# A column of 1e-9 behind the rows of scores, in fixed tiles, in a windowed attention with two MLPs

## The chip, the core and the metric

The kernel runs on one core of a Trainium2 chip. The metric is the device time of one execution in microseconds (us); the time of a version is the median of its runs. The core has five engines with instruction streams of their own: PE (TensorE, matrix products; its weight loads are listed as PEld), DVE (VectorE), ACT (ScalarE), POOL (GpSimd) and SP (SyncE, which here only issues DMAs). Each engine works through its stream in order, and an instruction that waits for another engine or for a DMA holds up all that stands behind it on its own engine.

## The reference

```python
scores = scale * np.matmul(q, k.transpose(0, 1, 3, 2))        # q, k, v: 4 x 8 heads x 576 x 64
mask_plain = (rel >= 0) & (rel < 32)                          # heads 0 to 3
mask_dil = (rel >= 0) & (rel < 128) & (rel % 4 == 0)          # heads 4 to 7
scores = np.where(masks, scores, -1e9)
scores = scores - np.max(scores, axis=-1, keepdims=True)
attn = np.exp(scores)
attn = attn / (np.sum(attn, axis=-1, keepdims=True) + 1e-09)  # the 1e-9 of this change
x = np.matmul(attn, v)                                        # as 2304 tokens x 512
h = x @ w_in;  x = np.maximum(0.01 * h, h) @ w_out            # 512 -> 2048 -> 512
a = x @ w1;  b = x @ w2;  out = ((a * b) @ w3) @ w_out2       # 512 -> 1024 -> 1024 -> 512
```

q and k are scaled up so that the scores spread widely. Inputs are float64 in memory, the output is float32.

## The kernel before

**Stages.** The attention is cut into 32 groups of rows, n = 0 to 31: two heads by one half of the 576 positions, which is 5 or 4 blocks of 64 queries, each against 96 keys (KB = 96). A group's scores are a tile s of 128 partitions by 5 (or 4) blocks by 96. The first MLP runs between the groups: hidden products (ps_h), Prelu on ACT into g, the split of g into two parts of reduced precision (gs: a CAST and a subtraction, line 116 and 118), and the product with w_out (ps_x). Behind the last groups, between the remaining parts of the first MLP, the second MLP's last two weights begin to be multiplied together (w3 by w_out2, products ps_wp).

**One group.** `score_steps` multiplies q by k (ps_s, L420), scales and masks into s (DVE, L435), takes the negated maximum nmax (DVE, L440), and then goes one of two ways. The 14 groups listed in ONE_EXP subtract the maximum on POOL (L443), take the exponential of the whole tile in one ACT instruction (L448), and sum the rows on DVE (L453). The other 18 take one ACT instruction for each block, with the maximum as bias, and ACT sums the row along the way (L456, accum_out). `normalize_steps` adds 1e-9 to the sums (DVE, L464), takes the reciprocal (DVE, L467) and multiplies s by it (POOL, L469). `turn_p` turns s with PE (ps_p, L485) and copies it to pT (L489), and `value_steps` multiplies by v (ps_o, L506) and writes x (L529, L532).

**Memory.** Tiles come from pools of SBUF, stacked from the left and from the right. `edge` is the outermost pool on the right and stays; before, it holds one unused tile of 96 bytes a partition. Inside it lies `att`: masks first (1,728 bytes a partition), then qT and kT (two each, 2,304 bytes), three slots for s (1,920 bytes each) and the small nmax, total and rec, then pT, v and nat. Slots of a tag are handed out in turn. Where the string START has the sign `^`, `att` is closed, and the pool `fold` is opened over the same bytes. Its first tiles are rawf (two slots of 4,096 bytes, raw words of w3), wo2f (two of 2,048 bytes, rows of w_out2), and wo2 (the split w_out2). A transfer or a write into such a tile waits for whatever last used the bytes under it.

**Order.** All of this up to the second MLP is issued by hand: every letter of the string START is one step of a stage, and every L takes the next letter of LOADS, which names a load for SP. So no scheduler moves anything; the order on each engine is that of the code. After `^` come seven loads: rawf0 and rawf1 (four DMAs each, L670) and then five of wo2f (L680). Of the steps behind, `p` is the CAST of wo2f into wo2 on ACT (L116) and `r` its remainder on DVE (L118); `0`, `1`, `2`, ... turn rawf into rf and w3T (POOL L113, ACT L165 and L167, DVE L154, L171 and L702, then ACT L116 and DVE L118); `W` is the product ps_wp; `H`, `g`, `c`, `l` are the hidden product, Prelu and split of the first MLP, and `J` its second product.

Of the kernel before, what the change touches and what calls it, by code (L numbers as in the profile page):

```python
# [8 lines left out]
F32 = mybir.dt.float32  # L9
# [8 lines left out]
ALU = mybir.AluOpType  # L18
AX = mybir.AxisListType
# [5 lines left out]
EPS = 1.0e-9  # L25
# [3 lines left out]
def tile_window_attention_two_mlps(  # L29
# [14 lines left out]
    nc = tc.nc  # L44
    P = 128
# [21 lines left out]
    QB, KB = 64, 96  # L67
    NQ = HS[0] // QB
# [5 lines left out]
    def pool(name, side):  # L74
        es = ExitStack()
        return es, es.enter_context(
            tc.tile_pool(name=name, bufs=1, side=side, reuse_waits="tile")
        )

    const = ctx.enter_context(tc.tile_pool(name="const", bufs=1, side="left"))  # L80
    edge = ctx.enter_context(tc.tile_pool(name="edge", bufs=1, side="right"))
    edge.tile([P, 24], F32, name="edge")
    psum_es = ExitStack()
    psum = psum_es.enter_context(tc.tile_pool(name="psum", bufs=1, space=PSUM, reuse_waits="tile"))
    win_es, win_p = pool("win", "left")
# [12 lines left out]
    def side_bank(name):  # L98
        return psum.tile([P, 512], F32, tag="side", name=name, bufs=2)
# [82 lines left out]
    ONE_EXP = (0, 1, 3, 6, 11, 13, 16, 17, 19, 20, 27, 28, 29, 31)  # L182
# [108 lines left out]
    def pair(pi):  # L291
        b, h0 = divmod(pi, HP)
        return b, 2 * h0, 2 * h0 < H // 2
# [60 lines left out]
    def first_key(i, plain):  # L354
        k0 = max(i * QB - WINDOW, 0)
        g0 = i * QB // SR * SR
        return k0 if plain else max(k0, g0)
# [47 lines left out]
        qk_t[nm, pi] = dst  # L405
        yield

    sm = {}

    def score_steps(n):  # L410
        pi, r = order[n]
        plain = pair(pi)[2]
        qt, kt = qk_t["q", pi], qk_t["k", pi]
        bl = R_BLOCKS[r]
        nb = len(bl)
        ps = side_bank(f"ps_s{n}")[:, : nb * KB].rearrange("p (i k) -> p i k", k=KB)
        for i in bl:
            for j in range(2):
                d = slice(j * D, (j + 1) * D)
                nc.tensor.matmul(  # L420
                    ps[j * QB : (j + 1) * QB, i - bl.start],
                    qt[d, i * QB : (i + 1) * QB],
                    kt[d, first_key(i, plain) : first_key(i, plain) + KB],
                    start=True, stop=True,
                )
        yield
        s = att.tile([P, NQ, KB], F32, tag="s", name=f"s{n}", bufs=3)[:, :nb]
        if plain:
            cut = 1 if r == 0 else 0
            spans = [(0, cut, masks[:, :cut])] if cut else []  # L430
            spans.append((cut, nb, masks[:, 1:2].to_broadcast([P, nb - cut, KB])))
        else:
            spans = [(0, nb, masks[:, bl.start : bl.stop])]
        for a, z, mk in spans:
            nc.vector.scalar_tensor_tensor(  # L435
                s[:, a:z], ps[:, a:z], SCALE, mk, op0=ALU.mult, op1=ALU.add
            )
        yield
        nmax = att.tile([P, NQ], F32, tag="nmax", name=f"nmax{n}", bufs=2)
        nc.vector.tensor_reduce(nmax[:, :nb], s, op=ALU.max, axis=AX.X, negate=True)  # L440
        yield
        if n in ONE_EXP:
            nc.gpsimd.tensor_tensor(  # L443
                s, s, nmax[:, :nb].unsqueeze(2).to_broadcast([P, nb, KB]), op=ALU.add
            )
        yield
        if n in ONE_EXP:
            nc.scalar.activation(s, s, AF.Exp)  # L448
            yield
        total = att.tile([P, NQ], F32, tag="total", name=f"total{n}", bufs=2)  # L450
        sm[n] = (s, total[:, :nb])
        if n in ONE_EXP:
            nc.vector.tensor_reduce(total[:, :nb], s, op=ALU.add, axis=AX.X)  # L453
            yield
        for i in range(nb):
            nc.scalar.activation(  # L456
                s[:, i], s[:, i], AF.Exp, bias=nmax[:, i : i + 1], accum_out=total[:, i : i + 1]
            )
        yield
        yield  # L460

    def normalize_steps(n):
        s, total = sm[n]
        nc.vector.tensor_scalar(total, total, EPS, None, op0=ALU.add)  # L464
        rec = att.tile([P, NQ], F32, tag="rec", name=f"rec{n}", bufs=2)
        nb = s.shape[1]
        nc.vector.reciprocal(rec[:, :nb], total)  # L467
        yield
        nc.gpsimd.tensor_tensor(  # L469
            s, s, rec[:, :nb].unsqueeze(2).to_broadcast([P, nb, KB]), op=ALU.mult  # L470
        )
        yield
# [833 lines left out]
    with ExitStack():  # L1306
        make_identity(nc, ident)
        att_es, att = pool("att", "right")
        mask_d = masks = att.tile([P, S // QB, KB], BF16, name="masks")
        nc.vector.memset(masks, 0.0)  # L1310
        def build_masks():


            def band(m, shift):
                for j in range(2):
                    mj = m[j * QB : (j + 1) * QB]
                    for base, sign in ((shift, 1), (WINDOW - 1 - shift, -1)):
                        nc.gpsimd.affine_select(
                            out=mj, in_=mj, compare_op=ALU.is_ge, fill=NEG, base=base,
                            pattern=[[-sign, KB]], channel_multiplier=sign,  # L1320
                        )

            shifts = [i * QB - first_key(i, False) for i in range(S // QB)]
            band(mask_d[:, 0], shifts[0])
            band(mask_d[:, 1], WINDOW)
            m = mask_d[:, 2:]
            nc.vector.tensor_copy(m, mask_d[:, 1:2].to_broadcast(list(m.shape)))
            for i in range(2, S // QB):
                if shifts[i] != WINDOW:
                    nc.vector.memset(mask_d[:, i], 0.0)  # L1330
                    band(mask_d[:, i], shifts[i])

                x = ((i * QB) // SR + 1) * SR - first_key(i, False)
                if x < KB:
                    for j in range(2):
                        mj = mask_d[j * QB : (j + 1) * QB, i, :x]
                        nc.gpsimd.affine_select(
                            out=mj, in_=mj, compare_op=ALU.is_ge, fill=NEG, base=x - shifts[i] - 1,
                            pattern=[[0, x]], channel_multiplier=-1,
                        )  # L1340
# [90 lines left out]
        def late_turn(i):  # L1431
# [4 lines left out]
            "TY": turn_rows,  # L1436
            "F": late_turn,
            "SMXqEw": score_steps,
            "RN": normalize_steps,
            "PC": turn_p,  # L1440
            "Vxy": value_steps,
# [17 lines left out]
        with tc.manual_schedule():  # L1459
            warm = bank2("warm")  # L1460
            build_masks()
            feed, QK = iter(LOADS), "0123456789ABCDEFGHIJKLMNOPQRSTUV"
            wo2_no = iter(range(NI * NI // NG))
            begun = {}
            for x in START:
# [38 lines left out]
                else:  # L1504
# [3 lines left out]
                    if at == 0:  # L1508
                        n = len(done[-1])
# [52 lines left out]
```

## Time and profile before

| | |
|---|---|
| median of 3 runs | 815.05 us (815.03 to 818.45) |
| the profiled execution | 814.0 us, span 812.2 us |
| mean granted TensorE clock | 0.999 |
| PE busy | 798.0 us, 98% of the span |
| DVE busy | 535.8 us, 66% |
| ACT busy | 418.2 us, 51% |
| POOL busy | 195.9 us, 24% |

The span runs from the first to the last instruction of the profiled execution; its own time is 1.8 us longer. All rows below are of this one execution. A row of a timeline gives the start in us, the duration in us (of all instructions, where it ends in x and a count), the engine, the line, the operation, the tile written and the tile read, and in square brackets the idle time of the engine just before and what ended it. SPq are the DMA issues on SP.

### The profile page before, as it was taken

The page shows a single profiled execution, that of the slowest core. Times are in us where ns is not written, and L with a number is a line of the kernel's source. Part 1 is how long each engine was busy: PE and PEld are TensorE (multiplying, and loading weights), DVE is VectorE, ACT ScalarE, POOL GpSimd, SP SyncE. Part 2 cuts the span into 40 slices and gives each one's busy share as a digit, 9 for nine tenths or more (in the row PEclk, how much of TensorE's full clock was granted, in tenths as well). Part 3 has the DMA queues.
Part 4 walks back from the last instruction along what each step waited for, and adds up shares of the span by engine and source line. Part 5 has one row for each costly group of instructions (what it writes and reads, how often), then busy time and mean ns, then how long its engine had stood idle before and what let it go on. Part 6 is the DMA issues. An engine that isn't in the chain of part 4 may idle for free.

```text
span 812.2 us, 16134 instructions
## 1 busy us (share of the span) xinstructions
PE 798.0 (98%) x5806; PEld 774.1 (95%) x5806; DVE 535.8 (66%) x1063; ACT 418.2 (51%) x954; POOL 195.9 (24%) x223
## 2 busy tenths in 40 slices
PE   8899999999999999999999999999999999999997
PEld 7799999999999999988989999999999999999997
DVE  4899997553555354567784777567869658466446
ACT  4799983452134352556664677554555235333341
POOL 4404421343332334431312210000110300121013
PEclk9999999999999999999999999999999999999999
DMA  6996846346552531477856789539999999889884
GB/s 154 254 322 210 258 116 187 94 143 174 136 155 68 136 102 27 131 175 216 241 174 232 258 277 302 200 112 338 358 382 375 304 305 308 253 253 284 301 253 89
DMA packets 162831, 175.79 MB, mean 216 GB/s; under 512 B 67520, under 2 KB 116160, under 8 KB 162752
## 3 DMA queue, kind: packets, MB, share of 16 engines
q1 hardware_dynamic: 158368, 173.69, 69.5%
q10 hardware_dynamic: 4384, 1.08, 0.6%
q8 instruction: 46, 0.75, 0.4%
q14 instruction: 33, 0.27, 0.1%
HBM read 137.89 MB, written 36.83 MB: 215 GB/s over the span
## 4 chain that ended last, share of the span: by engine, by line
PE 82%; ACT 5%; DVE 4%; SPq 3%; DMA 3%; issue 2%; POOL 0%; ACTq 0%; DVEq 0%; POOLq 0%
PE ps_x L126 7%; PE ps_h L126 7%; PE ps_x L127 7%; PE ps_x L128 7%; PE ps_h L127 7%; PE ps_h L128 7%; PE ps_b L127 3%; PE ps_b L126 3%; PE ps_b L128 3%; PE ps_s L420 2%; PE ps_o L506 2%; PE ps_a L126 2%; PE ps_a L127 2%; PE ps_a L128 2%; PE ps_p L485 2%
## 5 line engine op out<-in xcount | busy, mean ns | idle before, releaser
L126 PE MATMUL ps_h<-x,win 128*128 128x384 f32 (+2 forms) x440 | 139.5, 317 | 0.0
L128 PE MATMUL ps_h<-x,win 128*128 128x384 f32 (+2 forms) x440 | 137.5, 313 | 0.0
L127 PE MATMUL ps_h<-x,win 128*128 128x384 f32 (+2 forms) x440 | 137.5, 312 | 0.0
L126 PE MATMUL ps_x<-gs,wout 128*128 128x384 f32 (+2 forms) x356 | 114.5, 322 | 0.0
L128 PE MATMUL ps_x<-gs,wout 128*128 128x384 f32 (+2 forms) x356 | 112.4, 316 | 0.0
L127 PE MATMUL ps_x<-gs,wout 128*128 128x384 f32 (+2 forms) x356 | 112.4, 316 | 0.0
L118 POOL TENSOR_TENSOR gs<-g,gs 128x384 fp32r<-128x384 f32 (+2 forms) x69 | 65.8, 953 | 146.5 <-DVE gs L116 138.1
L577 ACT ACTIVATE g<-ps_h 128x384 f32<-128x384 f32 (+2 forms) x110 | 48.1, 438 | 100.6 <-PE ps_h L128 72.3
L126 PEld LDWEIGHTS ps_h<-x,win 128*128 128x128 f32 x440 | 83.1, 189 | 1.3
L127 PEld LDWEIGHTS ps_h<-x,win 128*128 128x128 f32 x440 | 83.1, 189 | 0.3
L128 PEld LDWEIGHTS ps_h<-x,win 128*128 128x128 f32 x440 | 83.1, 189 | 0.0
L118 POOL TENSOR_TENSOR p<-t,p 128x384 fp32r<-128x384 f32 x12 | 12.6, 1046 | 256.8 <-DMA place<-ws_dram 96.5
L126 PEld LDWEIGHTS ps_x<-gs,wout 128*128 128x128 f32 x356 | 67.1, 189 | 1.2
L127 PEld LDWEIGHTS ps_x<-gs,wout 128*128 128x128 f32 x356 | 67.2, 189 | 0.3
L128 PEld LDWEIGHTS ps_x<-gs,wout 128*128 128x128 f32 x356 | 67.1, 189 | 0.0
L116 DVE CAST gs<-g 128x384 fp32r<-128x384 f32 (+2 forms) x70 | 24.6, 352 | 57.7 <-PE ps_x L128 43.0
L456 ACT ACTIVATE s<-s,nmax 128x96 f32<-128x96 f32 x83 | 30.0, 364 | 21.8 <-DVE nmax L440 21.7
L127 PE MATMUL ps_b<-ys,place 128*128 128x384 f32 x120 | 40.2, 335 | 0.7 <-DVE ys L118 0.7
L126 PE MATMUL ps_b<-ys,place 128*128 128x384 f32 x120 | 40.1, 334 | 0.0
L128 PE MATMUL ps_b<-ys,place 128*128 128x384 f32 x120 | 40.1, 334 | 0.0
L435 DVE SCALAR_TENSOR_TENSOR s<-ps_s,masks 128x384 f32<-128x384 f32 (+2 forms) x40 | 19.8, 512 | 28.3 <-PE ps_s L420 27.9
L469 POOL TENSOR_TENSOR s<-s,rec 128x480 f32<-128x480 f32 (+1 forms) x32 | 30.0, 939 | 31.1 <-DVE rec L467 27.1
(253 smaller groups left out, 2115.9 us busy)
## 6 DMA issues: line engine op xcount, KB each, us to landing
place<-ws_dram SPq DMA_DIRECT2D x140, 256.0 KB
place<-wps_dram SPq DMA_DIRECT2D x84, 256.0 KB
ws_dram<-ws SPq DMA_DIRECT2D x24, 512.0 KB
raw<-in_moe_w_in_dram SPq DMA_DIRECT2D x16, 512.0 KB
raw<-in_moe_w_out_dram SPq DMA_DIRECT2D x16, 512.0 KB
rawf<-in_moe_w_dram SPq DMA_DIRECT2D x64, 128.0 KB
wo2f<-wo_dram SPq DMA_DIRECT2D x32, 256.0 KB
rawl<-in_moe_w_dram SPq DMA_DIRECT2D x16, 512.0 KB
```

Source lines behind the costliest of these rows:

```text
L116: copy_on(e_hi)(hi, src)
L118: e_lo.tensor_tensor(lo, src, hi.bitcast(F32), op=ALU.subtract)
L126: nc.tensor.matmul(ps, a[1], b[0], start=first, stop=False, skip_group_check=seeded)
L127: nc.tensor.matmul(ps, a[0], b[1], start=False, stop=False, skip_group_check=seeded)
L128: nc.tensor.matmul(ps, a[0], b[0], start=False, stop=last, skip_group_check=seeded)
L420: nc.tensor.matmul(ps[j * QB : (j + 1) * QB, i - bl.start], qt[d, i * QB : (i + 1) * QB], kt[d, first_key(i, plain) : first_key(i, plain) ...
L435: nc.vector.scalar_tensor_tensor(s[:, a:z], ps[:, a:z], SCALE, mk, op0=ALU.mult, op1=ALU.add)
L456: nc.scalar.activation(s[:, i], s[:, i], AF.Exp, bias=nmax[:, i : i + 1], accum_out=total[:, i : i + 1])
L469: nc.gpsimd.tensor_tensor(s, s, rec[:, :nb].unsqueeze(2).to_broadcast([P, nb, KB]), op=ALU.mult)
L485: nc.tensor.transpose(pss[g][:, i - i0], s[:, i], ident)
L506: nc.tensor.matmul(ps[j * D : (j + 1) * D, i * QB : (i + 1) * QB], vt[i][:, h + j, :], t[:, i, j * QB : (j + 1) * QB], start=True, stop=True,)
L577: nc.scalar.activation(g, ps, AF.Prelu, alpha=SLOPE)
```

## The change

A pad tile goes. Scores get three fixed tiles of 5 blocks by 97 columns, allocated right behind the masks, in place of three slots allocated when the first groups ask for them. Column 96 of each is set to 1e-9 once, by three POOL instructions. Where DVE sums (the 14 groups of ONE_EXP), its sum runs over 97 columns, and the separate addition of 1e-9 is gone. Where ACT sums (the other 18), 1e-9 is still added on DVE, now as a tensor from that column instead of a constant. total and rec move from `att` to `edge`.

```diff
-    edge.tile([P, 24], F32, name="edge")
...
-    sm = {}
+    sm, s_ring = {}, []
+
+    def score_ring():
+
+        for i in range(3):
+            s_ring.append(att.tile([P, NQ, KB + 1], F32, name=f"s_{i}"))
+            nc.gpsimd.memset(s_ring[i][:, :, KB:], EPS)
...
     def score_steps(n):
...
-        s = att.tile([P, NQ, KB], F32, tag="s", name=f"s{n}", bufs=3)[:, :nb]
+        t = s_ring[n % len(s_ring)]
+        s = t[:, :nb, :KB]
...
-        total = att.tile([P, NQ], F32, tag="total", name=f"total{n}", bufs=2)
+        total = edge.tile([P, NQ], F32, tag="total", name=f"total{n}", bufs=2)
         sm[n] = (s, total[:, :nb])
         if n in ONE_EXP:
-            nc.vector.tensor_reduce(total[:, :nb], s, op=ALU.add, axis=AX.X)
+            nc.vector.tensor_reduce(total[:, :nb], t[:, :nb], op=ALU.add, axis=AX.X)
...
     def normalize_steps(n):
         s, total = sm[n]
-        nc.vector.tensor_scalar(total, total, EPS, None, op0=ALU.add)
-        rec = att.tile([P, NQ], F32, tag="rec", name=f"rec{n}", bufs=2)
+        if n not in ONE_EXP:
+            eps = s_ring[n % len(s_ring)][:, : s.shape[1], KB]
+            nc.vector.tensor_tensor(total, total, eps, op=ALU.add)
+        rec = edge.tile([P, NQ], F32, tag="rec", name=f"rec{n}", bufs=2)
...
         mask_d = masks = att.tile([P, S // QB, KB], BF16, name="masks")
         nc.vector.memset(masks, 0.0)
+        score_ring()
+
         def build_masks():
```

On DVE, from the sum of group 1 to the reciprocal of group 2 (the number behind a name's last underscore is only a count), this stands before:

```order
L453 TENSOR_REDUCE total1_316<-s1_274 128x4
L464 TENSOR_SCALAR total1_316<-total1_316 128x4
L467 RECIPROCAL rec1_326<-total1_316 128x4
L435 SCALAR_TENSOR_TENSOR s2_328<-ps_s2_294,masks_101 128x480
L440 TENSOR_REDUCE nmax2_334<-s2_328 128x5
L404 COPY qT0_349<-ps_qT0_318 128x576
L435 SCALAR_TENSOR_TENSOR s3_366<-ps_s3_340,masks_101 128x384
L440 TENSOR_REDUCE nmax3_380<-s3_366 128x4
L404 COPY kT0_409<-ps_kT0_368 128x576
L464 TENSOR_SCALAR total2_354<-total2_354 128x5
L467 RECIPROCAL rec2_415<-total2_354 128x5
```

And in the same place of DVE after the change:

```order
L459 TENSOR_REDUCE total1_318<-s_1_104 128x4
L475 RECIPROCAL rec1_327<-total1_318 128x4
L441 SCALAR_TENSOR_TENSOR s_2_106<-ps_s2_297,masks_100 128x5x96
L446 TENSOR_REDUCE nmax2_334<-s_2_106 128x5
L403 COPY qT0_349<-ps_qT0_320 128x576
L441 SCALAR_TENSOR_TENSOR s_0_102<-ps_s3_340,masks_100 128x4x96
L446 TENSOR_REDUCE nmax3_379<-s_0_102 128x4
L403 COPY kT0_408<-ps_kT0_367 128x576
L472 TENSOR_TENSOR total2_354<-total2_354,s_2_106 128x5
L475 RECIPROCAL rec2_414<-total2_354 128x5
```

Group 1 (in ONE_EXP) has lost its addition, group 2 has it with a second tensor, and nothing else has moved; the rows of scores are now blocks of 96 with a gap (128x5x96) where they were one run (128x480).

On SP, where `fold` opens (the last load of v, then the first DMAs of rawf0 and rawf1, then wo2f; in brackets the semaphores that the issue waits for, DMAHW being those of earlier DMAs), this stands before:

```order
L381 DMA v13_4405<-in_v_dram 96x4x64 [waits DMAHW3_49]
L670 DMA rawf0_4631<-in_moe2_w3_dram 32x8x64 [waits DMAHW4_49,DVE_49]
...
L670 DMA rawf1_4636<-in_moe2_w3_dram 32x8x64 [waits DMAHW0_49]
...
L680 DMA wo2f_0_4641<-wo2_dram_91 128x512 [waits DMAHW4_49]
L680 DMA wo2f_1_4643<-wo2_dram_91 128x512 [waits DMAHW5_49,PE_49,Pool_49]
L680 DMA wo2f_2_4645<-wo2_dram_91 128x512 [waits DMAHW6_49,DMAHW4_49,DVE_49]
```

And after, in the same place of SP:

```order
L380 DMA v13_4367<-in_v_dram 96x4x64 [waits DMAHW3_49]
L678 DMA rawf0_4590<-in_moe2_w3_dram 32x8x64 [waits DMAHW4_49,PE_49,Pool_49]
...
L678 DMA rawf1_4595<-in_moe2_w3_dram 32x8x64 [waits DMAHW0_49]
...
L688 DMA wo2f_0_4600<-wo2_dram_90 128x512 [waits DMAHW4_49]
L688 DMA wo2f_1_4602<-wo2_dram_90 128x512 [waits DMAHW5_49]
L688 DMA wo2f_2_4604<-wo2_dram_90 128x512 [waits DMAHW6_49,DMAHW4_49,DVE_49]
```

No DMA has changed its place. The wait for PE and POOL has moved from the second wo2f, which was tenth in this row of loads, to the first DMA of rawf0, in place of its wait for DVE.

## Rows read from the trace of the kernel before

**Rows 1.** The page: busy time of the engines, and the chain by engine.

```profile
PE 798.0 (98%) x5806; PEld 774.1 (95%) x5806; DVE 535.8 (66%) x1063; ACT 418.2 (51%) x954; POOL 195.9 (24%) x223
...
PE 82%; ACT 5%; DVE 4%; SPq 3%; DMA 3%; issue 2%; POOL 0%; ACTq 0%; DVEq 0%; POOLq 0%
```

**Rows 2.** Stretches: start:end, length, busy time of each engine, clock, DMA.

```profile
40.00:330.00 290.00, 289.19 (x2673) 281.71 (x2667) 187.10 (x405) 152.28 (x403) 97.40 (x107) 1.00 0.53 151
330.00:350.00 20.00, 20.00 (x146) 19.33 (x146) 10.94 (x29) 10.40 (x27) 9.75 (x11) 1.00 0.60 152
350.00:800.00 450.00, 448.52 (x2516) 438.10 (x2515) 304.63 (x547) 231.08 (x451) 68.59 (x67) 1.00 0.81 265
```

**Rows 3.** Groups of line 464 on DVE: count, busy us, mean ns, idle before.

```profile
L464 DVE TENSOR_SCALAR total<-total 128x4 f32<-128x4 f32 x16 | 4.8, 302 | 1.6 <-ACT s L456 1.4
L464 DVE TENSOR_SCALAR total<-total 128x5 f32<-128x5 f32 x16 | 3.8, 237 | 5.6 <-ACT s L456 5.5
```

**Rows 4.** The chain that ended last, between 20 and 40 us.

```profile
27.73 9.81 DMA v<-in_v_dram
```

**Rows 5.** Waits of SP's queue: us in total, times, longest.

```profile
SPq L670 <- DVE s L435: 6.0, 1, 6.0
```

**Rows 6.** The timeline of SP's queue where fold opens.

```profile
327.34 3.77 SPq L670 DMA_DIRECT2D rawf<-in_moe_w_dram  x8
331.15 10.59 SPq L680 DMA_DIRECT2D wo2f<-wo_dram  x5
```

**Rows 7.** The timeline of PE: the last two groups turned, the first ps_wp.

```profile
332.25 0.71 PE L485 MATMUL ps_p<-ident,s 128*96 128x128 f32 x5
...
334.91 0.60 PE L485 MATMUL ps_p<-ident,s 128*96 128x128 f32 x4
...
349.31 0.47 PE L126 MATMUL ps_wp<-wo,w3T 128*128 128x512 f32 x1
```

**Rows 8.** The chain that ended last: two transfers of wo2f.

```profile
360.99 3.89 DMA wo2f<-wo_dram
...
408.09 3.24 DMA wo2f<-wo_dram
```

**Rows 9.** The timeline of ACT from 336 to 348 us.

```profile
336.03 0.63 ACT L116 CAST wo<-wo2f 128x512 fp32r<-128x512 f32 x1
...
339.77 0.63 ACT L116 CAST wo<-wo2f 128x512 fp32r<-128x512 f32 x1 [0.24 <-DMA wo2f<-wo_dram]
...
342.85 0.80 ACT L529 CAST x<-ps_o 128x96 fp32r<-128x96 f32 x4
345.36 0.49 ACT L577 ACTIVATE g<-ps_h 128x384 f32<-128x384 f32 x1 [1.71 <-PE ps_h L128]
...
347.83 0.61 ACT L116 CAST w3T<-rf 128x512 fp32r<-128x512 f32 x1
```

**Rows 10.** The timeline of DVE from 344 to 349 us.

```profile
344.23 0.68 DVE L171 CUSTOM_DVE_ANT_0 wf<-wf,rf 128x1024 uint16<-128x1024 uint16 x1
345.89 0.36 DVE L116 CAST gs<-g 128x384 fp32r<-128x384 f32 x1 [0.97 <-ACT g L577]
346.16 0.71 DVE L702 STREAM_TRANSPOSE rf<-wf 128x512 f32<-128x512 f32 x1
348.47 0.69 DVE L118 TENSOR_TENSOR w3T<-rf,w3T 128x512 fp32r<-128x512 f32 x1 [1.61 <-ACT w3T L116]
```

**Rows 11.** The timeline of POOL: the first reader of rawf.

```profile
339.14 1.71 POOL L113 TENSOR_SCALAR wf<-rawf 128x512 f32<-128x512 f32 x2
```

**Rows 12.** Stretches around PE's last matmul, in columns as above.

```profile
800.00:809.00 9.00, 7.03 (x41) 6.68 (x39) 6.24 (x12) 0.00 (x0) 1.66 (x2) 1.00 0.64 133
...
810.00:811.00 1.00, 0.00 (x0) 0.00 (x0) 0.00 (x0) 0.00 (x0) 0.00 (x0) 0.50 0.77 171
```

**Rows 13.** The timeline of PE at the start: warming products.

```profile
1.36 3.51 PE L1503 MATMUL warm<-ident 128*128 128x128 f32 x16 [1.36 <-POOL ident masks.py:199]
...
6.01 0.88 PE L1503 MATMUL warm<-ident 128*128 128x128 f32 x6
```

## The prediction

> **What bounds the kernel now.** I read the page first. PE is busy for 798.0 of 812.2 us and carries 82% of the chain that ended last; VectorE (DVE) carries 4% of it [rows 1]. So a change counts only as far as it makes PE stand still for longer or for less. The table of stretches then shows where PE stands still at all: from 40 to 330 us it is busy 289.19 of 290.00 us, from 330 to 350 us for all of 20.00, and behind that 448.52 of 450.00 [rows 2]. So PE has hardly anywhere to win back time: 0.81 us before 330, and 1.48 us behind 350. In the first 40 us PE does pause, and the chain there is one transfer of v of 9.81 us [rows 4], behind which neither a sum nor a reciprocal stands.
>
> Then I read, on each engine, what the change touches: the additions on DVE, and the place where the pool `fold` is opened over the bytes of `att`.
>
> **The removed additions.** All 32 cost DVE 4.8 + 3.8 = 8.6 us, 0.27 us each [rows 3]; the 14 that go are worth 14 x 0.27 = 3.8 us of DVE. Beside what are they? From 40 to 330 us DVE is busy for 187.10 of 290 us and PE for 289.19 [rows 2], so PE's work hides them, and PE's whole idle time there is 0.81 us; before 40 us the transfer of v hides them [rows 4]. I count 0. Were the cover gone, it would be the whole 3.8 us, which I keep as a bound.
>
> **The other 18 additions** read a column of 97-word pitch instead of a constant. No row shows this form. Below: no dearer than now, 0.24 to 0.30 us [rows 3]. Above: a tensor by tensor subtraction of 512 words takes 0.69 us [rows 10], 18 x (0.69 - 0.27) = 7.6 us of DVE at the very most. I take the nearer, 0, by the size of the tile; either way the third of its time that DVE idles from 40 to 330 us [rows 2] hides it. The same answer holds for the gap between rows of 96 on DVE, ACT and POOL, for the 97th word in the sums, and for the three settings of a column at the start, where PE only warms up.
>
> **The moved bytes.** This is the part that I price. `fold` begins with rawf0 and rawf1 (two times 4,096 bytes) and lies over the low end of `att`. Before, that end held masks (1,728 bytes) and the two qT and two kT (2,304 each); the slots of s began 10,944 bytes in, beyond both rawf. Now the three fixed tiles stand right behind the masks, so both rawf lie over them: the last use of rawf0's bytes was the scores of group 31 being read by DVE with qT and kT done, and becomes PE's turning of group 31's s. The order on SP says the same: the first rawf0 waited for DVE, and now waits for PE and POOL; the second wo2f has lost that wait.
>
> The trace has both events. SP waited 6.0 us at this DMA for DVE's L435 [rows 5] and issued it at 327.34 [rows 6]. The last turning (ps_p) runs from 334.91 to 335.51 [rows 7]; POOL's multiplication is ahead of it by necessity. So the issue goes from 327.34 to 335.5, +8.2 us. Queued behind it on SP, in order, are the other seven DMAs of rawf and all of wo2f.
>
> Who waits for these? First wo2f. wo2f_0 is issued 331.15 - 327.34 = 3.81 us behind rawf0 [rows 6], so at 339.3. Transfers of wo2f on the chain took 3.24 and 3.89 us [rows 8]; from 330 to 350 us the DMA share is 0.60 against 0.81 later [rows 2], so I take the shorter: it lands at 342.55 (343.2 by the longer). ACT takes it in the CAST at 336.03 [rows 9], in order, and everything behind it on ACT stands still: +6.5 us there (to +7.2).
>
> Next ACT goes on as before: the third wo2f is asked for when DVE has read the first, so that CAST (339.77, ended by that DMA) slides rigidly, and so do the conversions of rawf and the x of the last group (342.85 + 0.80 = 343.65) [rows 9]. rawf itself is no trouble: POOL reads it first at 339.14 [rows 11], and in the new order only once its neighbours arrive; ACT is later than it.
>
> Then slack is used up, twice. DVE's second L171 (ends 344.91) comes 6.5 later, at 351.4; the CAST behind it had idled 0.97 us for ACT [rows 10], so it comes only 5.5 later, and the turning L702 ends at 346.87 + 5.5 = 352.4. ACT's CAST of w3T began 0.96 us behind L702's end, at 347.83 [rows 9, 10]; ACT's two Prelus are now done by then (from 350.15), so it begins at 352.4: +4.6. DVE's remainder ends 349.16 + 4.6 = 353.75. PE's first ps_wp was at 349.31, 0.15 behind it [rows 7, 10], and has no more than that to give: it begins at about 353.8, **+4.5 us** (+5.2 by the longer transfer). PE stands still for this in one or two pieces (the hidden product at 343 may already wait for the held up Prelu), and it has no idle time behind 350 to give back but those 1.48 us [rows 2], so between 3.0 and 5.2 us reach the end.
>
> **A rule that could raise this.** PE ends its work in the stretch from 800 to 809 us, where it is still busy for 7.03 us at a granted clock of 1.00, that is at 2.4 GHz; it then has nothing to do, and from 810 to 811 us the granted clock is 0.50, the 1.2 GHz level [rows 12]. A stall of some 4 us in one piece is an idle time of the same order. Price, from rows: sixteen warming products at the start took 3.51 us, six of the same shape later 0.88 us, or 2.35 for sixteen [rows 13]; the loss until the engine is fast again was 1.2 us. The Trainium skill, TensorE: Matmul & The Clock Gate, Part 1: The HAM clock gate, says that the array falls to 1.2 GHz when idle and has to earn its full rate back by work; the end of this trace agrees, but no row before shows it in mid-kernel. By that rule the sum would be +5.7 instead of +4.5.
>
> **The sum.** 0 for the additions, 0 for the new forms, +4.5 us for the wait: 814.0 + 4.5 = 818.5 for an execution like the profiled one. The median of the runs, 815.05, stands 1.05 above that execution, so 819.5 for the median.
>
> **Rivals.**
> - *The wait is covered* (not slower). Place: the CAST of wo2f_0 on ACT. SP already runs 8.7 us ahead of ACT there (327.34 against 336.03), and POOL wants rawf only at 339.14. What decides is whether wo2f lands before ACT needs it: it would take a transfer that ends by 336.0, which an issue at 339.3 can't give, unless the wait for PE is met earlier than I think, by an earlier group's turning (the one before it ends at 332.25 + 0.71 = 332.96, 2.55 us sooner [rows 7]). Even then +5.6 at the issue leaves 2.55 us less than above at each step, +4.5 - 2.55 = 1.95 at the end: 817.0. Fully covered it is 815.0.
> - *The additions reach the end.* For: a held up addition delays the reciprocal, POOL and the turning, and PE does wait for that in places. Against: PE's 0.81 us of idle time from 40 to 330 us [rows 2]. It alone would give 815.05 - 3.8 = 811.3; with the wait, 815.7. It decides if DVE's sums end the chain in several groups.
> - *The clock falls in the stall.* For: the fall behind the last matmul [rows 12]. Against: the stall may come in two pieces. 815.05 + 5.7 = 820.75, with the longer transfer 821.5.
>
> **How the numbers follow.** My forecast, the wait alone, has a chance of 0.62, between 818.0 and 820.3; the clock 0.18; covered, wholly or in part, 0.14; the additions alone 0.06. About 0.5%, 4.1 us, is what a measurement of this kernel can tell from no change: slower begins at 819.1, faster at 811.0. The forecast lies close to that line, so I give 0.42 of its 0.62 to slower and 0.20 to the same; the clock is all slower; covered is all the same; of the additions 0.04 is faster (where the sums of 97 words or the new forms win something too) and 0.02 the same. That makes 0.60 slower, 0.36 the same, 0.04 faster. The range leaves out the wholly covered case, the additions alone and the last part of the clock: 816.2 to 821.8.
>
> **What would show it.** SP's wait at the first rawf ends with PE's ps_p, at about 335.5 instead of 327.3; ACT idles some 6 us before the CAST of wo2, ended by the DMA of wo2f; PE idles some 4 us in all between 343 and 354 us, before ps_h or ps_wp, the latter ended by DVE's w3T; behind that each stage starts about 4.5 us later. The additions are right at 0 if the turning of group 31 starts within 0.5 us of 334.91. I am wrong if rawf0 is still issued near 327, if ACT finds wo2f landed, if PE's idle time at 343 to 354 stays under 2 us, or if the stages from 354 to the end win more than 1.5 us back. A clock below 1.00 in the stretch behind the stall would show the third rival.

## The result, and the profile after

The changed kernel takes 823.78 us (median of 6 runs, 822.63 to 825.82) against 815.04 us (6 runs of before beside them): a ratio of 1.0109, interval 1.0092 to 1.0127. So it is slower, as forecast, but by 8.7 us (8.9 by the ratio), nearly twice the 4.5 that I had summed up, and above the top of my range (821.8). Run once more beside other experiments (e10) the ratio was 1.0127 (1.0109 to 1.0145). A ratio is estimated together with its interval and is not the quotient of the two medians; the two differ by up to 0.0008 here. Two of the twelve executions of e3, of 868 and 1307 us at a mean granted clock of 0.85 and 0.56, are left out of its ratio.

The profiled execution took 823.76 us, span 822.0. Up to the place where `fold` opens it was 0.8 us ahead of the one before: the last ps_p started at 334.11 instead of 334.91 [rows 7]. That lead belongs to the execution and not to the change (see e3 and e7), so I add 0.8 us wherever I compare times behind it.

The page and the waits of PE in the changed kernel (us in total, times, longest):

```profile
PE 801.9 (98%) x5806; PEld 776.4 (94%) x5806; DVE 537.3 (65%) x1049; ACT 417.6 (51%) x954; POOL 195.1 (24%) x226
...
PE ps_wp L125 <- DVE w3T L117: 4.8, 2, 4.3
PE ps_h L125 <- ACT g L585: 1.7, 1, 1.7
```

These are the two waits that the prediction put between 343 and 354 us. Every step on the way to them can be read. First SP: its waits, then the timeline of its queue, which answer to [rows 5, 6]:

```profile
SPq L678 <- PE ps_p L493: 14.1, 1, 14.1
...
334.78 3.77 SPq L678 DMA_DIRECT2D rawf<-in_moe_w_dram  x8
338.59 10.14 SPq L688 DMA_DIRECT2D wo2f<-wo_dram  x5
```

SP now waits for ps_p, and the first rawf goes out at 334.78 + 0.8, which is the 8.2 us later that was forecast. Next the transfers of wo2f on the chain that ended last, and ACT's timeline behind them, which answers to [rows 8, 9]:

```profile
338.59 4.37 DMA wo2f<-wo_dram
...
344.49 2.53 DMA wo2f<-wo_dram
```

```profile
334.69 0.64 ACT L497 COPY pT<-ps_p 96x384 f32<-96x384 f32 x2 [1.97 <-PE ps_p L493]
343.06 0.62 ACT L115 CAST wo<-wo2f 128x512 fp32r<-128x512 f32 x1 [7.73 <-DMA wo2f<-wo_dram]
...
347.04 0.62 ACT L115 CAST wo<-wo2f 128x512 fp32r<-128x512 f32 x1 [2.08 <-DMA wo2f<-wo_dram]
...
350.80 0.88 ACT L585 ACTIVATE g<-ps_h 128x384 f32<-128x384 f32 x2
353.50 0.62 ACT L115 CAST w3T<-rf 128x512 fp32r<-128x512 f32 x1 [1.83 <-DVE rf L710]
```

ACT stands still for 7.73 us until the first wo2f lands, 7.8 us later than before (343.06 + 0.8 against 336.03), where I had 6.5. DVE, which answers to [rows 10], with the POOL instruction beside its first conversion:

```profile
349.67 1.37 DVE L170 CUSTOM_DVE_ANT_0 wf<-wf,rf 128x1024 uint16<-128x1024 uint16 x1 [0.34 <-ACT rf L166]
...
351.85 0.67 DVE L170 CUSTOM_DVE_ANT_0 wf<-wf,rf 128x1024 uint16<-128x1024 uint16 x1
352.44 0.34 DVE L115 CAST gs<-g 128x384 fp32r<-128x384 f32 x1
352.71 0.70 DVE L710 STREAM_TRANSPOSE rf<-wf 128x512 f32<-128x512 f32 x1
354.15 0.69 DVE L117 TENSOR_TENSOR w3T<-rf,w3T 128x512 fp32r<-128x512 f32 x1 [0.74 <-ACT w3T L115]
...
349.48 1.02 POOL L117 TENSOR_TENSOR gs<-g,gs 128x384 fp32r<-128x384 f32 x1 [1.99 <-DVE gs L115]
```

And PE, which answers to [rows 7]:

```profile
334.11 0.60 PE L493 MATMUL ps_p<-ident,s 128*96 128x128 f32 x4
...
354.99 0.77 PE L125 MATMUL ps_wp<-wo,w3T 128*128 128x512 f32 x1 [4.35 <-DVE w3T L117]
355.55 0.63 PE L126 MATMUL ps_wp<-wo,w3T 128*128 128x512 f32 x1
355.98 0.63 PE L127 MATMUL ps_wp<-wo,w3T 128*128 128x512 f32 x1
...
359.82 0.58 PE L127 MATMUL ps_wp<-wo,w3T 128*128 128x512 f32 x1
360.24 0.33 PE L125 MATMUL ps_h<-x,win 128*128 128x384 f32 x1
```

The first ps_wp comes at 354.99 + 0.8 instead of 349.31, **6.5 us** late. Then something that my sum did not have: the ps_wp follow each other by 0.43 us (355.98 - 355.55) where they took 0.23 before. The stretches say why; the column behind POOL is the granted clock:

```profile
352.00:353.00 1.00, 0.00 (x0) 0.00 (x0) 1.00 (x3) 0.00 (x0) 0.13 (x1) 1.00 0.88 221
353.00:354.00 1.00, 0.00 (x0) 0.00 (x0) 0.41 (x1) 0.50 (x1) 0.86 (x1) 0.69 1.21 208
354.00:355.00 1.00, 0.01 (x1) 0.04 (x1) 0.69 (x1) 0.24 (x2) 0.35 (x1) 0.50 1.18 201
...
359.00:360.00 1.00, 1.00 (x4) 0.81 (x3) 0.69 (x1) 0.00 (x0) 0.15 (x1) 0.50 0.82 243
360.00:361.00 1.00, 1.00 (x7) 0.92 (x6) 0.00 (x0) 0.57 (x2) 0.00 (x0) 0.90 0.19 50
```

PE does nothing from 350.6 on; in 353 to 354 us the clock falls to the 1.2 GHz level, and it is back at 2.4 GHz only in 360 to 361. The twelve ps_wp, which all fall into this time, take 360.24 - 354.99 = 5.25 us; matched instruction by instruction with the trace of before they lose **2.4 us**. The Trainium skill (TensorE: Matmul & The Clock Gate, Part 1: The HAM clock gate) says that an idle array falls to 1.2 GHz; here the trace shows it in mid-kernel, which no row of before did.

So 6.5 + 2.4 = 8.9 us are lost at one place. From there to the end PE falls back by another 1.5 us, in small steps; about 1.0 of that became a finding of its own (e7).

### The profile page after: what moved, and what is told of

It reads as the page before. It is cut to its first block, busy times and chain, and to the rows that moved or that the text cites. A ratio compares the mean times of both kernels' runs of the same rounds, so it can differ in the third digit from the quotient of the medians.

```text
span 822.0 us, 16121 instructions
## 1 busy us (share of the span) xinstructions
PE 801.9 (98%) x5806; PEld 776.4 (94%) x5806; DVE 537.3 (65%) x1049; ACT 417.6 (51%) x954; POOL 195.1 (24%) x226
## 4 chain that ended last, share of the span: by engine, by line
PE 74%; DVE 10%; ACT 6%; DMA 4%; issue 3%; SPq 3%; POOL 0%; DVEq 0%; ACTq 0%; POOLq 0%
PE ps_x L125 6%; PE ps_h L125 6%; PE ps_x L127 6%; PE ps_x L126 6%; PE ps_h L127 6%; PE ps_h L126 6%; PE ps_b L126 3%; PE ps_b L125 3%; PE ps_b L127 3%; PE ps_s L425 2%; PE ps_a L125 2%; PE ps_a L126 2%; PE ps_a L127 2%; DMA wo2f<-wo_dram 2%; PE ps_o L514 2%
## 5 line engine op out<-in xcount | busy, mean ns | idle before, releaser
L117 DVE TENSOR_TENSOR wo<-wo2f,wo 128x512 fp32r<-128x512 f32 x32 | 25.2, 798 | 20.3 <-ACT wo L115 20.2
```

The costliest lines, as they stand in the source:

```text
L117: e_lo.tensor_tensor(lo, src, hi.bitcast(F32), op=ALU.subtract)
```

## Experiments

Two theories stood at the start. Theory 1: the moved bytes make SP wait, and what PE loses is stall and clock. Theory 2: the new form of rows and sums costs time in the attention itself. A third came from the traces of the first two runs. Ratios are to the kernel before, run on the same chip; its median was 813.25 us beside e1 to e4, 813.50 beside e6 to e9, 814.31 beside e10, e11, e12 and e5. A loss in us that stands behind a ratio is worked out from it.

**e1: the fixed tiles behind qT and kT, the rest of the change kept.**

```diff
-        score_ring()
...
+        if not s_ring:
+            score_ring()
         t = s_ring[n % len(s_ring)]
```

> The change with the three fixed tiles allocated behind qT and kT instead of right behind the masks; the column of 1e-9, the 97-word sums, the tensor additions and the moved total and rec all stay. If the moved bytes are the cause (theory 1), the first rawf is issued near 327 us again, ACT doesn't idle for wo2f, PE has no idle time between 340 and 355 us, the clock stays at 1.00 there, and the time is that of before or up to 1 us less: 814.0 to 815.3. If the rows with a gap, the 97th word or the second tensor cost the time (theory 2), it stays at 820 to 824. If each has a part, it lies between.

Measured: 815.31 us, ratio 1.0022 (1.0011 to 1.0034). SP and PE, in the timeline of its queue and in the stretch of the former stalls:

```profile
327.26 3.77 SPq L680 DMA_DIRECT2D rawf<-in_moe_w_dram  x8
...
340.00:355.00 15.00, 15.00 (x82) 14.01 (x82) 10.77 (x22) 9.38 (x19) 5.49 (x6) 1.00 0.64 152
```

The place of the tiles decides: no stall, clock 1.00, and about four fifths of the loss is gone. But the time is 1.8 us over before and not below it, so something else of the change costs a little.

**e2: only the place of the tiles, in the kernel before.**

```diff
-        s = att.tile([P, NQ, KB], F32, tag="s", name=f"s{n}", bufs=3)[:, :nb]
+        s = s_ring[n % 3][:, :nb]
...
         nc.vector.memset(masks, 0.0)
+        s_ring = [att.tile([P, NQ, KB], F32, name=f"s_{i}") for i in range(3)]
```

> The kernel before with nothing but three fixed tiles of 96 columns right behind the masks in place of the three slots; no column, all 32 additions as before. Theory 1 (moved bytes): SP issues the first rawf at about 335, PE idles about 1.7 us before ps_h and 4.3 us before ps_wp, the granted clock falls to 0.50 behind it, and the time is 8 to 10 us over before: 823 to 825. Theory 2 (the form of rows and sums): no change, 815.

Measured: 821.49 us, ratio 1.0100 (1.0079 to 1.0121), +8.1 us, and so below the 823 to 825 that I expected. PE's idle times in its timeline, and the clock in the stall and behind:

```profile
342.34 0.44 PE L126 MATMUL ps_h<-x,win 128*128 128x384 f32 x1 [0.92 <-ACT g L577]
...
353.15 0.47 PE L126 MATMUL ps_wp<-wo,w3T 128*128 128x512 f32 x1 [4.30 <-DVE w3T L118]
...
352.00:354.00 2.00, 0.84 (x4) 0.75 (x5) 1.14 (x3) 1.24 (x3) 1.10 (x2) 1.00 0.87 171
354.00:356.00 2.00, 2.00 (x7) 1.52 (x6) 1.75 (x3) 1.08 (x2) 1.00 (x1) 0.50 0.18 53
```

One edit that adds and removes no instruction repeats nearly all of the loss: theory 1 holds from both sides. The stall is 5.6 us here (by the matched starts of PE's instructions), the clock 1.6. The clock falls later than in the changed kernel: it stays at 1.00 through the 4.30 us in which PE idles, and falls at 354.0, when PE has been at work again for 0.85 us. So the first ps_wp still follow each other by 0.23 us and only seven by 0.43, which is why the clock costs less here.

**e3: the kernel before without the 14 additions.**

```diff
-        nc.vector.tensor_scalar(total, total, EPS, None, op0=ALU.add)
+        if n not in ONE_EXP:
+            nc.vector.tensor_scalar(total, total, EPS, None, op0=ALU.add)
```

> The kernel before without the addition of 1e-9 in the 14 groups where DVE sums (left out there, not done elsewhere); nothing else. My prediction's step (covered by PE and by the transfer of v): no change, within 0.3 us of before. The rival step (the 0.8 us that the changed kernel is ahead of before at 330 us is these additions): 0.5 to 1.0 us faster, 814.1 to 814.5, PE's ps_p of the last group 0.8 us earlier. All of their busy time reaching the end would be 3.8 us, 811.3.

Measured: 813.96 us, ratio 1.0004 (0.9993 to 1.0014). The additions are worth nothing, and PE at 330 us was not ahead but 0.5 us behind. The 0.8 us lead was the execution's: over all profiles it lies between 1.75 us ahead (e2, which has all additions) and 0.97 behind (e12, which lacks the 14). The sign that the prediction had set for the additions, a last turning within 0.5 us of 334.91, was therefore too fine: the changed kernel missed it, at 334.11, and so did e7, which has all additions, at 334.09.

**e4 and e8: PE kept at work in the longer stall.** Products of the identity are written into the bank of the first ps_wp, ahead of it (30 in e4, 13 in e8):

```diff
             wp_ps[g] = [side_bank(f"ps_wp{g}_{x}") for x in range(NG)]
+            if g == 0:
+                for _ in range(30):
+                    nc.tensor.matmul(wp_ps[g][0][:, :P], ident, ident, start=True, stop=True)
```

> The changed kernel with 30 products of the identity by itself put into the bank of the first ps_wp just ahead of it, so that PE works on through the longer of its two stalls; what they write is overwritten. By the warming products of before (0.15 us each) they take 4.4 us, about the 4.35 us that PE idles there. If 2.4 us of the loss is the clock (theory 1 with the clock), the twelve ps_wp behind take 0.23 us each instead of 0.43, the granted clock stays at 1.00, and the time falls by 2.0 to 2.5 us to 821.3 to 821.8. If the ps_wp are slow for another reason (their own waits or their weight loads), it stays at 823.8 or gets longer.

Measured: 825.12 us, ratio 1.0139 (1.0117 to 1.0161): no gain. The filling was too long, since I took the warming products as one instruction each: 30 products are 60 instructions, and the first had to wait for its bank until 351.17, so that ps_wp began at 357.86. But they then followed each other by 0.23 us, at a clock of 1.00. Hence e8:

> As e4, with 13 products of the identity instead of 30. In e4 they could start only when the bank was free (351.2) and were 60 instructions of 0.11 us, 6.9 us, so that they ran 3.5 us past the end of the stall; the ps_wp behind took 0.23 us each at a clock of 1.00. 13 products are 26 instructions or 2.9 us and end at about 354.1, before w3T comes at 354.9. If the clock cost 2.4 us in the changed kernel, it is 1.5 to 2.5 us faster than that (ratio to before 1.008 to 1.009 against 1.0109). If the fall of the clock doesn't hinge on PE's idleness there, ps_wp take 0.43 us again and the time stays.

Measured: 821.62 us, ratio 1.0102 (1.0080 to 1.0123): by itself undecided against 1.0109. In its timeline of PE the effect is plain:

```profile
350.53 3.14 PE L726 MATMUL ps_wp<-ident 128*128 128x128 f32 x26 [0.98 <-DVE x L540]
353.77 0.50 PE L125 MATMUL ps_wp<-wo,w3T 128*128 128x512 f32 x1
354.11 0.39 PE L126 MATMUL ps_wp<-wo,w3T 128*128 128x512 f32 x1
354.34 0.39 PE L127 MATMUL ps_wp<-wo,w3T 128*128 128x512 f32 x1
```

So it was run again on one chip with the changed kernel.

**e10 and e11: the changed kernel and e8, side by side** (no new edit).

> The changed kernel itself, once more beside the three below on one chip. It should repeat 1.0109 of before (1.009 to 1.013), PE's two stalls (1.7 and 4.3 us) and the clock at 0.50 behind the second.

> The kernel of e8 once more, now on the same chip as the changed kernel. In e8's trace the twelve ps_wp took 0.23 us each (2.4 us less than in the changed kernel), but PE then waited 0.7 us more at a later ps_wp. If the clock is a term of its own: 1.2 to 2.5 us faster than the changed kernel, ratio to before 1.0080 to 1.0095. If the slow ps_wp only fill time in which PE would wait for ACT's and DVE's conversions anyway: under 0.5 us faster.

Measured: 824.92 us for the changed kernel, ratio 1.0127 (1.0109 to 1.0145), and 821.90 with the filling, 1.0088 (1.0070 to 1.0106). By the medians the filling wins 3.0 us, though it does no work that is needed: the clock is a term of its own. It is a little over the 2.4 of the trace and the top of what I expected, but the two intervals are wide enough for 1 to 5 us. In the two traces the way from the last ps_p to the last matmul differs by 2.9 us, and 2.4 of them lie in the twelve ps_wp; PE does not wait longer behind them instead (between the changed kernel's first trace and e8's it does, by 1.1 us).

**e7: only total and rec moved, in the kernel before.** In the traces of e1 and of the changed kernel PE's matmuls from 430 us on stand a few ns further apart, 0.95 us in sum; in those of e2 and e3 they don't. What e1 and the change share is that the outer pool holds 128 bytes instead of 96, so that rawf, ys (the operands that the second MLP's products stream), yf and all other tiles of the later pools on the right stand 32 bytes lower (by the built programs the first ys is at 189,280 instead of 189,312; the old addresses are multiples of 64).

```diff
-    edge.tile([P, 24], F32, name="edge")
...
-        total = att.tile([P, NQ], F32, tag="total", name=f"total{n}", bufs=2)
+        total = edge.tile([P, NQ], F32, tag="total", name=f"total{n}", bufs=2)
...
-        rec = att.tile([P, NQ], F32, tag="rec", name=f"rec{n}", bufs=2)
+        rec = edge.tile([P, NQ], F32, tag="rec", name=f"rec{n}", bufs=2)
```

> The kernel before with only total and rec moved into the outer pool in place of the pad tile, which puts the later pools on the right 32 bytes lower; three slots of s, all additions and the order as before. Theory 3 (the shift): 1.0 to 1.8 us over before (ratio 1.0012 to 1.0022), small distances after 430 us +0.95 us. Its rival: no change.

Measured: 815.82 us, ratio 1.0022 (1.0006 to 1.0039). The same two matmuls of the second MLP, in the timeline of PE of the kernel before:

```profile
599.71 0.33 PE L128 MATMUL ps_a<-ys,place 128*128 128x384 f32 x1
...
787.04 0.33 PE L126 MATMUL ps_b<-ys,place 128*128 128x384 f32 x1
```

and of e7:

```profile
598.16 0.34 PE L127 MATMUL ps_a<-ys,place 128*128 128x384 f32 x1
...
786.10 0.34 PE L125 MATMUL ps_b<-ys,place 128*128 128x384 f32 x1
```

Between them lie 187.33 us before and 187.94 in e7. Over all fourteen profiles this distance is 187.91 to 187.94 in the seven with the shift (the change twice, e1, e4, e7, e8, e11) and 187.32 to 187.35 in the seven without it (before, e2, e3, e5, e6, e9, e12). Nothing falls between. From the last ps_p to the last matmul e7's trace is all the same not longer than that of before (0.1 us shorter), because small waits elsewhere are shorter by as much; that the shift costs time rests on the runs of e7 and on e1 against e6.

**e6 and e9: the 32 bytes taken back**, in e1 and in the changed kernel, with total and rec as slices of one tile of 80 bytes:

```diff
+    small = edge.tile([P, 4, 5], F32, name="small")
...
+        total = small[:, n % 2]
...
+        rec = small[:, 2 + n % 2]
```

> The kernel of e1 (fixed tiles behind qT and kT, all else of the change kept) with total and rec as slices of one tile, so that the outer pool takes 96 bytes again and every tile of the later pools on the right stands where it stood before; in e1 and in the changed kernel they all stand 32 bytes lower. In the traces of both, PE's matmul to matmul distances from 430 us on are longer by 0.95 us in sum, in steps of some ns, and in those of e2 and e3, which don't shift, by 0. Theory 3 (the 32 bytes cost 1 us or more in the second MLP): 1.0 to 1.8 us less than e1's ratio of 1.0022, that is 1.0000 to 1.0010 of before, and the small distances after 430 us add up to 0 against before. Its rival (the gap between rows, the second tensor or the 97th word cost it in the attention): it stays at 1.0022.

Measured: 813.83 us, ratio 1.0007 (0.9993 to 1.0020). With both causes gone, everything else of the change (97-word sums, the gap between rows, 18 additions of two tensors, 14 additions fewer) is no measurable change.

> The changed kernel with total and rec as slices of one tile, so that only the 32 bytes of the shift are taken back; the fixed tiles stay right behind the masks. Theory 3: 1.0 to 1.8 us less than the changed kernel, ratio to before 1.009 to 1.0097 against 1.0109, stall and fall of the clock as in the changed kernel. Its rival: 1.0109.

Measured: 821.34 us, ratio 1.0096 (1.0073 to 1.0119), as expected, though its interval reaches the 1.0109 of the change. The stall is 5.7 us, and the clock falls to 0.50 in it as in the changed kernel; here it is back within the twelve ps_wp, and costs 1.9 us.

**e12: e9 with the first two wo2f issued ahead of rawf**, all addresses kept.

```diff
                     conv3 = conv3_jobs()
+                    make = conv3.raw_tile
+                    first = [make(i) for i in range(2)]
+                    conv3.raw_tile = lambda i: first[i] if i < 2 else make(i)
...
-            "UVmnyyzzzzzyyy
+            "UVmnzzyyzzzyyy
```

> The kernel of e9 (the changed kernel with the 32 bytes taken back, fixed tiles right behind the masks), with the first two wo2f issued ahead of the two rawf; all tiles keep their addresses, and rawf0 still waits for the turning of group 31. If what hurts is wo2f standing behind rawf on SP (my chain): wo2f is issued near 327 again, ACT takes it without waiting, PE has no stall over 1 us at 343 to 355, the clock stays at 1.00, and the ratio to before falls from 1.0096 to between 0.9995 and 1.003. If the late rawf alone would hold ps_wp up as much: still over 1.006.

Measured: 816.11 us, ratio 1.0022 (1.0013 to 1.0031). In ACT's timeline and PE's:

```profile
337.00 0.63 ACT L116 CAST wo<-wo2f 128x512 fp32r<-128x512 f32 x1
...
344.09 0.62 ACT L116 CAST wo<-wo2f 128x512 fp32r<-128x512 f32 x1 [3.60 <-DMA wo2f<-wo_dram]
...
352.04 0.47 PE L126 MATMUL ps_wp<-wo,w3T 128*128 128x512 f32 x1 [1.66 <-DVE w3T L118]
```

ACT takes the first wo2f without waiting; the third, still behind rawf, comes later and leaves a stall of 1.66 us (over the 1 us that I expected), in which the clock stays at 1.00. The late rawf is in this kernel as well and costs at most that. What hurts is the queue on SP: wo2f behind a DMA that waits.

**e5: the kernel before without any addition.**

```diff
-        nc.vector.tensor_scalar(total, total, EPS, None, op0=ALU.add)
```

> The kernel before without any of the 32 additions of 1e-9 (left out; a row's sum is at least 1 there, so that 1e-9 is below the last bit of it). If additions are covered (as e3 shows for 14 of them, ratio 1.0004): no change, 0.9985 to 1.0010. If those of the other 18, each ahead of a reciprocal that POOL waits for, count: up to 2 us less, 0.9975. It is the one version here that could beat the kernel before.

Measured: 813.94 us, ratio 1.0000 (0.9985 to 1.0015). Not even all 32 are worth anything, and no version here beats the kernel before.

## Why the prediction was wrong

**The additions, the new forms: 0.** Right: e3, e5 and e6 lie at 1.0004, 1.0000 and 1.0007.

**The moved bytes, as far as SP.** Right in place, cause and size: SP waits for PE's ps_p, +8.2 us at the first rawf; e1 and e2 show the cause by taking it away and by adding it alone, e12 that the order on SP carries it.

**From SP to PE: "+4.5 us".** This term was too small. It measured 6.5 us in the changed kernel's trace (6.2 in that of e10), 5.6 in that of e2 and 5.7 in that of e9. The step "I take the shorter" failed first: the transfer took 4.37 us, not 3.24, so that ACT's CAST was 7.8 us late and not 6.5. From its issue to the CAST it took from 3.35 (e9) to 4.47 us in the seven profiles where wo2f stands behind the late rawf (e2, e4, e8, e9, e11 and two of the changed kernel). That the second wo2f now goes out right behind the first (it has lost its wait) may lengthen it; this was not tried apart. Second, "slides rigidly" was off: the third wo2f took 0.2 us longer, and DVE's first L170 took 1.37 us, with POOL's subtraction beside it (349.48 to 350.50), where it had taken 0.69 in the profile that I read; 0.35 us of this reached the second L170. That part is no effect of the change: in 13 of the 14 profiles, e1, e3, e5, e6 and e7 among them, POOL's subtraction begins first and DVE takes 1.37 to 1.50 us, and the profile of before is the exception. The slack that I counted was there and was used up, 0.97 and about 0.9 us: 7.8 + 0.2 + 0.35 - 1.0 - 0.9 = 6.45.

**The clock: a rival at 0.18, priced at 1.2 us.** It belonged in the likeliest case. "The stall may come in two pieces" was true and no help, for the longer piece is 4.35 us, and in all four profiles with such a piece and nothing to fill it (two of the change, e2, e9) the clock fell in it or, in e2, just behind it. The price came from the products at the start of the kernel, 1.2 us; here twelve ps_wp stand behind the stall, and all of them run at the 1.2 GHz level: 2.4 us in both traces of the change, 3.0 by e11 against e10, and 1.6 and 1.9 us in e2 and e9, where some of the twelve ran at full rate.

**The 32 bytes: not in the sum at all.** I saw total and rec move and the pad go, and read only which bytes are reused by whom. The pad of 96 bytes, which nothing reads, was what held the tiles on the right on multiples of 64, the ys of the second MLP among them. Its loss costs 1.0 us in PE's matmuls, 1.8 us (0.5 to 3.2) by the runs of e7.

Together: e9 (stall and clock) 7.8 us, e7 (shift) 1.8, e6 (all else) 0.6, not clear of 0. That is 9.6 to 10.2 us, where the change itself measured 8.9 and 10.3 by its two ratios.

## What to carry to other kernels

When tiles change their place, ask which transfer reuses their bytes next, and then what stands behind that transfer on its queue: here a wait that no one needed early held up a load that the next engine took in order. The stalls of 4.3 to 4.7 us on PE had the clock as a second term in every profile here that left them empty, at half rate over the matmuls that came next (1.6 to 2.4 us), and not where other products filled them (e4, e8, e11). And an unused tile may be there for the address of all that lies below it.

## What was not expected of the hardware

Products that stream an operand 32 bytes lower ran slower, by 187.94 to 187.33 us over the same stretch of the second MLP, 0.3%. Which operand it is can be read from where the time is lost. The second MLP works in three passes. In the built programs the ys that most products of the first and the third pass stream lie in a pool on the right, on multiples of 64 bytes before and on odd multiples of 32 in e7; the ys of the second pass and all weights (place, ws) lie in pools on the left, at the same addresses in both. The third pass, in the timeline of PE of the kernel before:

```profile
701.93 0.33 PE L127 MATMUL ps_a<-ys,place 128*128 128x384 f32 x1
...
790.33 0.33 PE L127 MATMUL ps_ay<-p,place 128*128 128x384 f32 x1
```

and of e7:

```profile
700.51 0.34 PE L126 MATMUL ps_a<-ys,place 128*128 128x384 f32 x1
...
789.40 0.33 PE L126 MATMUL ps_ay<-p,place 128*128 128x384 f32 x1
```

This stretch takes 88.40 us in the seven profiles without the shift and 88.90 in the seven with it. From 613.4 to 701.9 us, where the second pass streams its ys, all fourteen agree within 0.02 us. So it is the streamed operand that counts here. But it isn't every matmul: the ps_wp behind the first twelve, both of whose operands were shifted in the same way, lose nothing, and in the attention, where qT, kT, pT and v stand on odd multiples of 32 in e7 too, the matched distances from 40 to 345 us differ by under 0.05 us in sum (waits left out). A shifted weights operand by itself was not tried.

DVE's first L170 and POOL's subtraction meet in every profile, and the one that begins second is the longer one: in 13 profiles POOL begins 0.08 to 0.19 us ahead, and DVE takes 1.37 to 1.50 us; in the profile of before DVE begins 0.11 us ahead and takes 0.69, and POOL takes 1.47 us where it has 1.01 to 1.03 in the others. POOL's times are the less exact ones, and no run took one of the two away.
